# Block-sparse attention and GELU MLP in one kernel: a written-out order, other turns of batch 0's keys and queries, and second-batch loads without holds

## The chip, the cores and the metric

The kernel runs on one core of one Trainium2 chip. The metric is device time in microseconds (us). Instructions are named by their engine: PE (TensorE, matrix products), DVE (VectorE), ACT (ScalarE), POOL (GpSimd) and SP (SyncE, which here only starts transfers). L1124 is line 1124 of the kernel before; the changed file is shorter, and its lines are named only where the text says so.

## The reference

Four batches of eight heads, 768 positions and 64 elements per head go through an attention in which each query sees its own block of 64 keys and the best three others, causally. The rows of all heads then go through an MLP with a tanh GELU.

```python
def _attn_ref(q, k, v):                       # (4, 8, 768, 64)
    k_rep = k.reshape(B, H, n_blocks, block, D).mean(axis=3)      # 12 blocks of 64
    gate_scores = np.einsum('bhsd,bhnd->bhsn', q, k_rep)          # masked causally
    top_idx = np.argsort(gate_scores, axis=-1)[..., -top_k:]      # top_k = 3
    ...                                       # mask: chosen blocks and the own one, causal
    scores = np.where(mask, scale * np.matmul(q, k.transpose(0, 1, 3, 2)), -1e9)
    attn = softmax(scores)
    return np.matmul(attn, v)

def _moe_ref(x, w_in, w_out):                 # x (3072, 512), w_in (512, 2048), w_out (2048, 512)
    h = x @ w_in
    g = 0.5 * h * (1.0 + np.tanh(c * (h + 0.044715 * h * h * h)))
    return g @ w_out
```

## The kernel before

The work is cut into 16 pairs of heads, four pairs to a batch. The program first writes down every step as an `Op` with the engines that may run it, an estimated duration on each, the steps that it depends on, and the buffers that it takes and gives. `Plan.solve` then plays these through in an order of priority (the table `RANK`, one number for each step), chooses engine and buffer, and the instructions are issued in the order that comes out. Each engine runs its own instructions strictly in that order.

The steps of a pair of heads are these.

- `load` and `load_0` bring q, k and v on SP's queue. Usually rows of 64 floats (256 bytes) are read. In the other form, `emit_t` at L427, pieces of 32 floats (128 bytes) are read, laid out so that DVE's stream transpose (L585) can finish turning the tile. Batch 0 uses the first form for k and for the queries of pairs 0 and 1, and the second form for the queries of pairs 2 and 3 (`TURN`); every later batch uses the second form for k and q.
- `pre` makes the turned keys and queries, the sums of the keys of each block, and the gate. In batch 0 a key tile is turned by an ordinary fp32 product with an identity that has two more columns, of ones in each half (`identk`, 130 columns, L566); the two more columns give the block sums, and one multiplication (L603) puts them in place. A query tile is turned by the transposing form of the same instruction (L569, 128 columns). The gate is L693 on PE, followed on DVE by a small transpose and the four lines L716, L725, L726, L730 that choose the blocks. The choice is turned by PE (L762) and copied beside the queries as a mask.
- `heads2` (batch 0) and `heads` (later batches) are the attention: products with the mask in them (L866, L1049), exponentials on ACT (L885, L1062), the causal cut on POOL (L911, L1076), products with v (L934, L1088), division (L953, L972), and a turn of the result into `xT` (L991, L996).

For each batch, `s1` makes the hidden layer (L1124 on PE, GELU on ACT at L1136). For batch 0 `s2_plain` makes the second layer (L1206); for later batches `s2` makes it with seven products in place of eight (L1254). The first product of `s1(0)` needs the first half of w_in and the last exponentials of batch 0.

`load_w` starts the transfers of w_in and w_out, two halves each, on POOL's queue at L485. `hold` is a transfer of 16 elements from a weight tile on SP's queue (L493). SP's queue stops at it until that half of the weights has landed, and so the loads behind it start late: the first hold stands ahead of k and q of pair 4, the second ahead of v of pair 4 and everything of pair 5 and later pairs. On SP's queue each transfer also waits until the eighth transfer before it has landed.

`warm` gives 72 products of an identity with itself (L1401), of lowest priority, which the plan puts wherever it believes PE to be idle.

Of the kernel before, what the change touches and what calls it, by code (L numbers as in the profile page):

```python
# [20 lines left out]
RANK = [  # L21
    143, 420, 146, 147, 145, 418, 121, 260, 475, 56, 260, 228, 112, 261,
    587, 70, 261, 497, 19, 324, 5, 4, 324, 6, 2, 323, 8, 631, 1, 326, 32,
    54, 326, 31, 24, 324, 16, 758, 3, 329, 20, 42, 329, 13, 337, 326, 40,
    367, 372, 329, 30, 355, 38, 955, 1277, 846, 49, 934, 948, 573, 141, 248,
    583, 1191, 645, 590, 118, 241, 117, 242, 240, 198, 61, 119, 83, 613,
    108, 900, 357, 89, 751, 650, 150, 88, 253, 252, 148, 388, 1017, 1315,
    1018, 986, 109, 50, 36, 362, 473, 27, 204, 130, 22, 28, 712, 129, 23,
    21, 832, 236, 135, 265, 286, 124, 209, 428, 151, 520, 230, 325, 351,
    954, 235, 327, 350, 901, 624, 328, 433, 1099, 552, 310, 939, 305, 97,  # L30
    375, 529, 318, 882, 317, 417, 374, 889, 330, 285, 363, 287, 69, 233,
    595, 174, 137, 595, 90, 176, 339, 384, 339, 95, 111, 256, 898, 581, 441,
    280, 110, 897, 629, 923, 227, 474, 352, 298, 258, 543, 921, 62, 259,
    660, 142, 626, 829, 316, 510, 131, 216, 710, 276, 160, 26, 187, 282,
    321, 366, 189, 526, 208, 277, 533, 257, 185, 949, 431, 429, 494, 430,
    577, 331, 268, 641, 278, 838, 381, 625, 273, 289, 320, 462, 237, 465,
    369, 461, 730, 171, 464, 359, 341, 436, 458, 264, 358, 348, 1512, 269,
    456, 364, 398, 937, 213, 432, 361, 365, 360, 864, 460, 251, 219, 639,
    281, 354, 272, 347, 909, 234, 535, 344, 899, 340, 338, 370, 307, 127,
    218, 760, 387, 373, 243, 217, 791, 98, 379, 378, 945, 353, 186, 839,  # L40
    416, 478, 371, 776, 523, 956, 380, 138, 591, 524, 175, 343, 229, 488,
    170, 349, 801, 445, 840, 482, 12, 199, 65, 491, 595, 309, 564, 37, 79,
    85, 80, 84, 713, 17, 1128, 1069, 1232, 283, 284, 1228, 43, 41, 134, 313,
    1093, 1138, 1143, 1171, 755, 9, 559, 314, 400, 579, 288, 477, 466, 476,
    522, 15, 415, 444, 446, 521, 11, 1071, 504, 413, 1094, 25, 585, 512,
    602, 592, 94, 1070, 621, 841, 1072, 7, 593, 530, 528, 642, 14, 489,
    1114, 1319, 484, 10, 578, 414, 409, 485, 39, 493, 471, 454, 499, 18,
    549, 859, 861, 560, 34, 684, 734, 952, 1073, 35, 636, 596, 1102, 677,
    48, 496, 857, 447, 486, 29, 1235, 1257, 1269, 1286, 165, 1248, 778, 990,
    1198, 1220, 1217, 1218, 1223, 308, 203, 291, 211, 190, 715, 721, 1230,  # L50
    51, 172, 1226, 1266, 503, 565, 534, 681, 767, 676, 576, 822, 678, 652,
    653, 759, 770, 786, 612, 536, 911, 787, 792, 793, 800, 916, 917, 1043,
    1249, 126, 125, 222, 293, 295, 303, 292, 300, 226, 158, 689, 690, 736,
    743, 817, 836, 965, 404, 195, 192, 391, 395, 545, 546, 702, 423, 201,
    757, 421, 424, 425, 377, 691, 693, 718, 762, 735, 563, 495, 479, 505,
    541, 519, 619, 1124, 487, 194, 1237, 729, 246, 247, 245, 244, 249, 498,
    584, 427, 383, 604, 795, 794, 1061, 1213, 412, 746, 630, 932, 1321, 440,
    434, 270, 91, 907, 401, 768, 123, 634, 63, 796, 720, 104, 212, 798, 802,
    651, 675, 1040, 72, 724, 896, 46, 1044, 919, 254, 605, 223, 1039, 106,
    615, 294, 667, 744, 178, 668, 774, 924, 597, 68, 1329, 597, 87, 662,  # L60
    597, 173, 205, 52, 53, 81, 82, 77, 396, 76, 773, 989, 531, 86, 78, 918,
    74, 107, 385, 144, 221, 386, 159, 816, 664, 225, 356, 844, 833, 177,
    977, 392, 163, 692, 183, 782, 834, 301, 181, 154, 940, 835, 179, 740,
    393, 164, 705, 402, 538, 890, 335, 599, 103, 156, 599, 115, 169, 599,
    132, 162, 33, 73, 601, 616, 666, 459, 71, 688, 513, 483, 665, 719, 845,
    149, 255, 197, 188, 399, 502, 196, 714, 302, 567, 166, 726, 722, 304,
    206, 622, 75, 394, 506, 128, 717, 716, 306, 224, 765, 723, 290, 220,
    707, 403, 514, 673, 764, 537, 698, 262, 600, 96, 550, 600, 140, 334,
    600, 116, 167, 64, 555, 994, 974, 161, 263, 553, 544, 202, 184, 500,
    501, 728, 297, 59, 210, 279, 518, 152, 312, 1127, 618, 122, 1274, 1216,  # L70
    623, 136, 319, 1214, 406, 1126, 480, 368, 322, 733, 139, 1260, 457,
    1215, 938, 271, 470, 114, 661, 410, 1019, 155, 935, 481, 953, 927, 933,
    1264, 603, 790, 812, 903, 566, 250, 930, 902, 654, 426, 606, 725, 761,
    699, 1666, 872, 1341, 883, 1541, 1060, 1023, 992, 1062, 1645, 928, 904,
    922, 942, 1373, 950, 1063, 1088, 1007, 1178, 711, 685, 814, 819, 1663,
    1542, 92, 448, 905, 1067, 655, 1090, 1101, 1547, 818, 913, 910, 929,
    1394, 1064, 1032, 1029, 1068, 1139, 1056, 1053, 975, 1097, 1182, 468,
    451, 453, 925, 1049, 1013, 1059, 1066, 885, 1006, 1001, 875, 876, 101,
    1225, 914, 1356, 1425, 1275, 1100, 1112, 1255, 1227, 1137, 467, 442,
    881, 912, 1098, 1492, 1494, 1491, 1469, 1579, 1649, 804, 450, 463, 1144,  # L80
    1675, 1766, 1751, 1459, 1605, 1609, 1607, 920, 1689, 1688, 1278, 1389,
    1452, 1468, 1641, 1710, 961, 1680, 1660, 1683, 1697, 967, 737, 749, 100,
    1696, 1754, 1009, 1011, 784, 1031, 1033, 1016, 1025, 1024, 1020, 1132,
    1095, 1045, 1131, 1140, 1146, 1147, 1046, 1221, 1262, 1276, 1263, 777,
    750, 1239, 1241, 1080, 659, 656, 772, 1243, 1083, 695, 979, 57, 779,
    783, 1118, 1160, 754, 1158, 1219, 1298, 1324, 886, 1014, 1440, 1516,
    669, 511, 382, 469, 443, 1209, 570, 753, 868, 1152, 1245, 1314, 703,
    1409, 1538, 1424, 1421, 1461, 1458, 1672, 113, 267, 105, 180, 982, 1771,
    200, 982, 1772, 232, 982, 1775, 342, 299, 58, 60, 207, 67, 539, 93, 828,
    452, 397, 66, 969, 527, 848, 1351, 870, 133, 588, 1642, 1156, 988, 1212,  # L90
    1700, 1606, 991, 1429, 1699, 1698, 1092, 1057, 1010, 1048, 1608, 727,
    1581, 1455, 1578, 1177, 1244, 1532, 1496, 1175, 960, 1602, 936, 617,
    968, 1183, 1366, 1047, 157, 983, 1769, 231, 983, 1768, 756, 983, 1770,
    311, 405, 120, 274, 275, 438, 532, 408, 657, 1234, 492, 906, 435, 542,
    849, 866, 865, 644, 878, 1580, 1206, 1258, 1681, 1390, 1065, 1291, 1701,
    1682, 1194, 1159, 1740, 1026, 1717, 1190, 1419, 1021, 1661, 908, 803,
    1117, 1456, 1106, 1236, 1121, 999, 620, 998, 1089, 996, 1406, 830, 984,
    1773, 558, 984, 1774, 594, 984, 1776, 1489, 411, 437, 1724, 1723, 449,
    407, 873, 877, 884, 1332, 1204, 871, 389, 850, 966, 1005, 419, 895,
    1008, 1353, 1304, 1261, 1224, 1290, 915, 658, 1012, 1203, 1355, 780,  # L100
    1085, 1129, 855, 888, 1240, 1022, 1229, 1523, 1242, 1145, 856, 887, 788,
    1084, 825, 1030, 1289, 860, 1113, 747, 985, 1778, 556, 985, 1777, 540,
    985, 1767, 748, 1331, 1323, 1515, 1514, 1345, 820, 1346, 1526, 957, 962,
    1352, 1326, 731, 853, 1081, 1082, 672, 1252, 607, 1551, 1335, 1015,
    1201, 1561, 507, 1438, 1120, 1256, 1313, 1483, 1125, 1310, 1322, 1312,
    571, 1296, 1325, 1433, 785, 1437, 1119, 1420, 752, 1055, 1155, 1671,
    1259, 1493, 568, 569, 1270, 1272, 1422, 1684, 697, 831, 808, 869, 1611,
    943, 947, 1037, 1036, 1079, 813, 811, 810, 944, 1728, 1674, 1704, 1695,
    1714, 1104, 993, 1096, 1179, 1736, 1115, 1189, 1135, 1136, 1726, 1300,
    1308, 1306, 1318, 1676, 1170, 1168, 1165, 1172, 1721, 1207, 1635, 980,  # L110
    976, 1038, 1111, 1105, 1103, 562, 1233, 1148, 1163, 1281, 1544, 1134,
    1133, 1161, 1166, 1722, 1173, 1002, 1091, 1162, 1693, 1707, 963, 964,
# [55 lines left out]
class Op:  # L168
    def __init__(self, engines, emit, deps, prio, takes=None, gives=(),
# [5 lines left out]
        self.takes = ([] if takes is None else  # L175
                      [takes] if isinstance(takes, tuple) else takes)
        self.gives = gives
        self.lag = lag
        self.end = None


# [98 lines left out]
def kernel(  # L280
# [55 lines left out]
    NK = 3  # L336
# [1159 lines left out]
```

## Time and profile before

| | |
|---|---|
| three runs | 257.35, 258.61, 259.38 us; median 258.61 |
| span of the profiled execution | 257.8 us, granted clock 1.00 |
| PE, DVE, ACT, POOL busy | 250.8, 179.6, 165.2, 86.3 us |
| L1401, the fillers | 72 on PE |
| first and last product of real work on PE | L566 at 5.03 us, L1254 until 254.15 us |
| first L1124 of batch 0 | 39.58 us |
| DMA | 32.63 MB; SP's queue q1 27.62 MB, the weights' queue q0 4.19 MB |

The profile records one execution. The table of times has no separate time for that execution, so its own time is read from the span: the span runs from the first instruction to the last, and the median of the runs is 0.8 us above it. A product on PE is recorded with its way through the array, so that a PE that is called busy can hide idle time of up to a few tenths of a microsecond; the distance from one start to the next shows more. Times inside the span are counted from its start.

### The profile page before, as it was taken

To read this page: it belongs to the slowest core of one execution; us is meant where nothing else is said; L and a number is where in the kernel's file an instruction comes from. 1 tells how busy PE (TensorE), PEld (TensorE's weight loads), DVE (VectorE), ACT (ScalarE), POOL (GpSimd) and SP (SyncE) were. 2 spreads that over 40 slices of the span, in tenths; PEclk is the share of its full clock that TensorE was granted. 3 is DMA by queue.
4 is the path that set the end of the run, shared out by engine and by line. 5 is a ranking of instruction groups with operands and counts; after the bars stand their busy time and mean duration, and the time that the engine had idled before them with its cause. 6 is when DMAs were issued, how large, how long until landed. Compare 5 with 4: busy or idle time off the path is not lost.

```text
span 257.8 us, 6491 instructions
## 1 busy us (share of the span) xinstructions
PE 250.8 (97%) x2530; PEld 174.8 (68%) x2530; DVE 179.6 (70%) x523; ACT 165.2 (64%) x207; POOL 86.3 (33%) x169
## 2 busy tenths in 40 slices
PE   6799999998999999999999999999999999999997
PEld 5676776564556556556678876556778796667886
DVE  2887863318478999999999999997844462227552
ACT  2359688564789996565989587565898953664000
POOL 8754834003355676223043835100143310000000
DMA  8997898999969997899599694222011152000222
GB/s 159 218 152 161 152 215 132 186 225 185 206 132 212 161 196 159 154 188 174 86 206 194 113 215 99 66 69 51 1 75 42 41 104 83 3 0 0 84 81 84
DMA packets 134095, 32.63 MB, mean 127 GB/s; under 512 B 127696, under 2 KB 130096, under 8 KB 134064
## 3 DMA queue, kind: packets, MB, share of 16 engines
q1 hardware_dynamic: 129328, 27.62, 54.5%
q0 software_dynamic: 3136, 4.19, 10.0%
q10 hardware_dynamic: 1600, 0.39, 0.8%
q8 instruction: 20, 0.33, 0.5%
q14 instruction: 11, 0.09, 0.1%
HBM read 27.26 MB, written 6.29 MB: 130 GB/s over the span
## 4 chain that ended last, share of the span: by engine, by line
PE 71%; DMA 11%; DVE 7%; SPq 7%; ACT 2%; issue 2%; POOL 0%; DVEq 0%; ACTq 0%
PE bank L1254 21%; PE wide L1124 18%; PE wide L1049 10%; PE bank L1206 7%; SPq L427 6%; PE bank L1088 6%; DMA ksd<-in_k_dram 5%; DMA w_in<-in_moe_w_in_dram 4%; PE bank L1401 3%; PE bank L693 2%; DMA qsd<-in_q_dram 2%; PE wide L866 1%; ACT at L885 1%; PE bank L566 1%; DVE sel L725 1%
## 5 line engine op out<-in xcount | busy, mean ns | idle before, releaser
L1124 PE MATMUL wide<-xT,w_in 128*128 128x384 f16 x512 | 87.2, 326 | 0.1
L1136 ACT ACTIVATE G<-wide 128x768 f16<-128x768 f32 x64 | 51.8, 810 | 41.7 <-PE wide L1124 41.7
L1124 PEld LDWEIGHTS <-w_in 128*128 128x128 f16 x512 | 49.3, 98 | 33.2 <-issue 1.9
L1062 ACT ACTIVATE at<-wide 128x896 f16<-128x896 f32 x72 | 63.3, 917 | 10.5 <-PE wide L1049 8.1
L1076 POOL TENSOR_SCALAR_AFFINE_SELECT at<-at 128x256 f16<-128x256 f16 x72 | 31.1, 433 | 66.4 <-ACT at L1062 65.9
L1049 PE MATMUL wide<-qT,kT 76*128 76x512 f16 (+3 forms) x192 | 38.7, 305 | 0.0
L393 POOL CAST kT<-k 64x768 f16<-64x768 f32 x21 | 18.1, 862 | 37.4 <-DVE k L585 30.4
L1254 PE MATMUL bank<-w_out,G 128*128 128x256 f16 x216 | 30.0, 272 | 0.0
L1254 PEld LDWEIGHTS <-G 128*128 128x128 f16 x288 | 26.9, 98 | 4.1
L1298 DVE TENSOR_TENSOR osb<-bank,osb 128x512 f32<-128x512 f32 (+1 forms) x38 | 22.5, 596 | 8.8 <-PE bank L1254 8.2
L1206 PE MATMUL bank<-w_out,G 128*128 128x512 f16 x96 | 25.8, 379 | 0.0
L1088 PEld LDWEIGHTS <-at 128*128 128x128 f16 x504 | 21.6, 98 | 4.3 <-POOL at L1076 0.4
L885 ACT ACTIVATE at<-wide 128x1024 f16<-128x1024 f32 (+3 forms) x24 | 20.8, 917 | 5.5 <-PE wide L866 5.4
L1049 PEld LDWEIGHTS <-kT 76*128 76x128 f16 x192 | 17.5, 98 | 9.7
L1088 PE MATMUL bank<-v,at 128*128 128x65 f16 x504 | 23.8, 194 | 0.0
L1254 PEld LDWEIGHTS <-XS 128*128 128x128 f16 x216 | 20.3, 98 | 3.1 <-issue 0.3
L1254 PE MATMUL bank<-TS,XS 128*128 128x256 f16 x144 | 20.6, 272 | 0.0
L585 DVE STREAM_TRANSPOSE k<-ksd 128x768 f32<-128x768 f32 x12 | 11.6, 969 | 10.2 <-DMA ksd<-in_k_dram 10.2
L1194 DVE TENSOR_TENSOR XS<-G 128x768 f16<-128x768 f16 x12 | 6.5, 550 | 15.2 <-ACT G L1136 15.0
L1401 PE MATMUL bank<-ident 128*128 128x256 f16 x72 | 12.8, 302 | 2.1 <-DVE ident L323 2.1
L972 DVE TENSOR_TENSOR xn<-bank,zr 128x384 f16<-128x384 f32 x24 | 13.4, 558 | 0.8
L1206 PEld LDWEIGHTS <-G 128*128 128x128 f16 x96 | 8.7, 98 | 7.6 <-issue 1.0
(97 smaller groups left out, 322.8 us busy)
## 6 DMA issues: line engine op xcount, KB each, us to landing
out_dram<-osb SPq DMA_DIRECT2D x23, 256.0 KB, 2.0
vsd<-in_v_dram SPq DMA_DIRECT2D x26, 192.0 KB, 3.2
qsd<-in_q_dram SPq DMA_DIRECT2D x48, 96.0 KB, 2.5
ksd<-in_k_dram SPq DMA_DIRECT2D x48, 96.0 KB, 2.5
w_in<-in_moe_w_in_dram POOLq DMA_DIRECT2D x2, 1024.0 KB, 10.7
w_out<-in_moe_w_out_dram POOLq DMA_DIRECT2D x2, 1024.0 KB, 12.5
G<-in_k_dram SPq DMA_DIRECT2D x4, 192.0 KB, 4.6
G<-in_v_dram SPq DMA_DIRECT2D x4, 192.0 KB
```

The costliest lines, as they stand in the source:

```text
L393: nc.gpsimd.tensor_copy(out=out, in_=in_)
L885: nc.scalar.activation(out=T["at", u][:, :, 0:n], in_=plan.buf[("st",) + u].rearrange("p (h w) -> p h w", h=2)[:, :, 0:n], func=AF.Exp, bi ...
L1049: nc.tensor.matmul(st[:, x:e], kT16[i][h][0:76, s0:s0 + 128], qT16[i][h][0:76, s0 + (x - cb):s0 + (e - cb)], start=True, stop=True)
L1062: nc.scalar.activation(out=T["at", u][:, 0:n], in_=plan.buf[("st",) + u][:, 0:n], func=AF.Exp, bias=0.0, scale=SCALE)
L1076: nc.gpsimd.affine_select(out=dg, in_=dg, compare_op=ALU.is_ge, fill=0.0, base=0, pattern=[[0, 2], [1, 128]], channel_multiplier=-1)
L1088: nc.tensor.matmul(pvv[:, qc, 0:65], at[:, cb + (qc - jc) * 128: cb + (qc - jc + 1) * 128], v16[i][:, jc, h, :], start=(gi == 0 and jc == ...
L1124: nc.tensor.matmul(hps[:, 512 * e:512 * e + HALF], w_in16[:, ci, (2 * j + e) * 128: (2 * j + e + 1) * 128], T["xT", b][:, ci, HALF * h:HAL ...
L1136: nc.scalar.activation(out=G[:, :, h, j, :], in_=plan.buf["hps", b, j, h].rearrange("p (e w) -> p e w", e=2)[:, :, 0:HALF], func=AF.Gelu_a ...
L1206: nc.tensor.matmul(plan.buf["ops", b, ti], G[:, f % 2, 2 * ti // NC, f // 2, ti % (NC // 2) * 128:ti % (NC // 2) * 128 + 128], w_out16[:, ...
L1254: nc.tensor.matmul(dst[:, HD * h:HD * h + HD], FACT[m][0][:, j, t * 128:(t + 1) * 128], FACT[m][1][:, j, :], start=(clear and j == 0), sto ...
L1298: nc.vector.tensor_tensor(out=dst(), in0=src(), in1=other(), op=ALU.add)
L1401: nc.tensor.matmul(plan.buf["warm", n][:, 0:256], ident16, z, start=True, stop=True)
```

## The change

`RANK` and `Plan.solve` are gone. In their place stand a list of all steps in the order of issue (`ORDER`), a list of the buffers to take (`BUFFER`), and, for 37 steps, ACT, and for 20 steps, POOL, as the engine; every other step runs on the first engine that it names. Of the 72 fillers `ORDER` names 32: 13 ahead of the first product of real work, 19 after it, and none after the last.

The counts of instructions change in these places. Queries of pairs 2 and 3 are loaded in rows of 64 floats and turned by PE (12 products of 128 columns more; two DVE stream transposes and four SP transfers fewer). Keys of pairs 2 and 3 are turned by the transposing form (12 products of 128 columns in place of 12 of 130), and their block sums are made on DVE by four reductions of 128x384 and four multiplications in place of four multiplications. Five of the eight copies of turned keys go from DVE to ACT and one mask copy goes from ACT to DVE; two copies of queries are added on ACT and two on DVE. The two holds are gone; the second half of w_in and w_out now wait for loads of pairs 4 and 5, by a small copy on POOL that reads them.

```diff
-    TURN = {"k": (), "q": (2, 3), "v": ()}
+    TURN = {"k": (), "q": (), "v": ()}
+    KSUM = (0, 1)
...
-                    if key == "k":
+                    if key == "k" and p in KSUM:
                         nc.tensor.matmul(w[:, c * 130:(c + 1) * 130], src,
                                          identk, start=True, stop=True)
                     else:
                         nc.tensor.transpose(w[:, c * 128:(c + 1) * 128], src,
                                             ident32)
...
+                    if p not in KSUM:
+                        half = slice(6 * a, 6 * a + 6)
+                        nc.vector.tensor_reduce(
+                            out=ks[:, half],
+                            in_=plan.buf["wk", p, a][:, 0:HALF].rearrange(
+                                "p (n w) -> p n w", w=64),
+                            op=ALU.add, axis=AXL.X)
+                        for x in into:
+                            nc.vector.tensor_tensor(
+                                out=x[:, :, half], in0=bmask[:, :, 0:6],
+                                in1=ks[:, half].unsqueeze(1).to_broadcast(
+                                    [128, 2, 6]), op=ALU.mult)
+                        return
...
-    def solve(self):
...
+    def run(self):
+        engine = {n: e for e, ops in ENGINE.items() for n in ops}
+        picks = iter(BUFFER)
+        for n in ORDER:
+            op = self.ops[n]
             for kind, key in op.takes:
+                if key not in self.buf:
+                    self.buf[key] = self.kinds[kind][0][next(picks)]
+            op.emit(engine.get(n, next(iter(op.engines))))
...
-    def load_w(name, dst, src, part, deps, prio, after=None):
+    def load_w(name, first, dst, src, parts, prio, after):
         def emit(_):
+            x = const.tile([1, 16], FP32, name=f"after_{name}_{first}")
+            nc.gpsimd.tensor_copy(out=x, in_=T[after][0:1, 0, 0, 0:16]
...
+            for part in parts:
+                nc.gpsimd.dma_start(out=dst[part], in_=view[part])
-    def hold(name, src, dep):
-        def emit(_):
-            x = const.tile([1, 16], FP16, name=f"held_{name}")
-            nc.sync.dma_start(out=x, in_=src[0:1, 0, 0:16])
-        return add({SP: 0.5}, emit, [dep], prio=-1)
...
+    load_w("in", 0, w_in16, moe_w_in, ins[:1], -200, ("v", 3))
+    for p in (HP, HP + 1):
+        for key in ("k", "q", "v"):
+            load(p, key, issued["v" if p == HP else "q", 3 if p == HP else HP])
+    load_w("in", 1, w_in16, moe_w_in, ins[1:], -100, ("q", HP))
+    load_w("out", 0, w_out16, moe_w_out, outs, 40, ("k", HP + 1))
```

The order on each engine changes nearly everywhere. What the text below uses of it is this. On SP the ten loads of pairs 1 to 3 are followed at once by k and q of pair 4, k of pair 5 and v of pair 4, then six of the eight small `fill` transfers, v and q of pair 5, the last two fills, q and k of pair 6, k of pair 7. On POOL the first half of w_in is started after the cast of pair 3's queries and of its v; the second half after 15 of the 17 causal cuts of batch 0; w_out after all 17 and after the cast of pair 4's v. On DVE the stream transposes of k and q of pair 4 and k of pair 5 stand among the last steps of batch 0, ahead of the last copy of `xT`. On PE the gate of pair 4 stands ahead of `s1(0)`, the gate of pair 5 right behind the first two products of the second layer, and attention of pair 4 follows seven products of the second layer after the end of `s1(0)`.

## The prediction

> **What bounds the kernel now.** I read the page first, then the busy time of each engine in stretches of ten us, then the timelines of PE, ACT, DVE and SP where the stretches point.
>
> ```profile
> span 257.8 us, 6491 instructions
> PE 250.8 (97%) x2530; PEld 174.8 (68%) x2530; DVE 179.6 (70%) x523; ACT 165.2 (64%) x207; POOL 86.3 (33%) x169
> ```
>
> PE has the least room. Since its records overlap, I also took the distances from one start to the next: L1124 has 163 ns for 384 columns, L1254 109 ns for 256, L1206 216 ns for 512, each at its smallest value nearly always. From 62 us to 254 us PE therefore has nothing to give but its work. The stretches (busy us of each engine in ten) say where time is left.
>
> ```profile
> 10.00:20.00 10.00, 7.89 (x109) 6.03 (x107) 8.78 (x39) 5.35 (x9) 4.99 (x8) 1.00 1.09 173
> ...
> 50.00:60.00 10.00, 9.34 (x58) 5.39 (x56) 2.66 (x4) 6.44 (x8) 1.51 (x2) 1.00 1.30 213
> 60.00:70.00 10.00, 9.49 (x60) 4.96 (x61) 6.19 (x21) 5.59 (x8) 2.13 (x4) 1.00 1.06 198
> 70.00:80.00 10.00, 10.00 (x106) 5.58 (x104) 7.40 (x25) 8.49 (x12) 6.69 (x12) 1.00 0.76 151
> ```
>
> So the change can win in two places: in batch 0's attention, before the first L1124 at 39.58 us, and in the hole about 60 us. After that the end follows at a fixed distance: last product at 254.15, then one addition, one store and its landing, 3.65 us to the end of the span.
>
> In batch 0's attention no engine is full; ACT, with 24 exponentials, is the longest chain.
>
> ```profile
> 14.20 1.52 ACT L885 ACTIVATE at<-wide 128x512 f16<-128x512 f32 x2
> ...
> 39.43 1.02 ACT L885 ACTIVATE at<-wide 128x1024 f16<-128x1024 f32 x1
> 40.47 1.28 ACT L832 ACT_TABLE_LOAD   x1
> ```
>
> From 14.20 to 40.47 are 26.3 us; the L885 rows in between add up to 20.9, so ACT waits 5.4 us, each time for L866, which waits for a mask. The hole at 60 us is one late load:
>
> ```profile
> 36.30 0.57 SPq L493 DMA_DIRECT2D held_in<-w_in  x1
> 36.91 4.63 SPq L427 DMA_DIRECT2D qsd<-in_q_dram  x4
> 41.59 2.24 SPq L427 DMA_DIRECT2D ksd<-in_k_dram  x4
> ```
>
> ```profile
> 57.31 0.98 DVE L585 STREAM_TRANSPOSE k<-ksd 128x768 f32<-128x768 f32 x1 [10.16 <-DMA ksd<-in_k_dram]
> ```
>
> ```profile
> 60.51 0.48 PE L693 MATMUL bank<-q,ksb 128*32 128x160 f32 x8 [1.18 <-DVE ksb L645]
> ```
>
> The hold keeps SP until 36.30; k of pair 4 is started at 41.59 and lands at 57.3, and PE waits 1.34 us (start to start) for its gate. The packet records tell why it took 14 us: while w_out flows, the two queues take turns one for one (48 to 50 us: 370 packets of 1 KB from q0 and 370 of 128 bytes from q1), where q1 alone moves 1300 packets of 128 bytes per us.
>
> **The change part by part.** I work with the time from the first L1124 to the end, 257.8 - 39.58 = 218.2 us, and with the moment at which it starts.
>
> *Turning.* L566 costs two records of 112 ns for each of 12 products, 2.7 us; L569 has one of 109 ns, so keys of pairs 2 and 3 cost 1.3 us. The 12 new query turns cost 1.3 us. PE gains 0.1 us, in a stretch where it waits anyway: nothing. On DVE two transposes (0.97 each) and five key copies (0.55) go, 4.7 us; two query copies (1.1), a mask copy (0.55) and four reductions come. L628 sums 768 columns in 0.95 us, so half as many take 0.5 (bounds 0.25 and 0.95), 2.0 in all: DVE gains about 1 us. ACT gains work: of its copies five of 0.48 us, 2.4 in all, now stand between the exponentials.
>
> *First exponential.* Before, DVE makes both gate transposes and copies for both halves of pair 0 ahead of L716 at 9.38. After, the first half's gate needs only its own k and q, and runs before the second half's turn of q: 7.4 in place of 8.27. The mask comes 0.8 us earlier; the two copies on ACT between mask and exponential take it no further back. First exponential 13.35 in place of 14.20.
>
> *ACT's chain.* 13.35 + 20.9 + 2.4 = 36.6 without a wait. The first L1124 needs the buffer of the last exponential but one, 0.4 earlier: 36.2. With all 5.4 us of old waits: 41.6. Following the masks, pair 2's is copied at about 25.3 for an exponential that could start at 25.8, so that product and latency leave 0.6 of wait, and pair 3's at 31.1 leaves 0.5. The late waits of 1.2, 0.7 and 0.4 us before L885 came from the queries turned on DVE (L585 at 27.71) and the gate at 30.06; they go. I take 1.5 us: 37.7.
>
> *First half of w_in.* POOL starts it behind the cast of pair 3's queries, which needs ACT's last query copy. On ACT that is after 9.9 us of exponentials and 2.4 of copies: 13.35 + 12.3 + 0.6 of wait = 26.3. Two casts and the small copy (0.82 + 0.84 + 0.19) make 28.2; before, the trigger was at 27.06 and the half landed at 36.28, 9.2 later. I get 37.4, and 0.8 more for q1's packets in between (26 ns beside 173 for one of 2 KB): 38.2. So the weights set the start of `s1(0)`, at 38.2 (36.8 if ACT never waits and nothing is shared): 1.4 us earlier than 39.58.
>
> *Loads without holds.* q1 moves 870 packets of 256 bytes per us. Counted on from 14 us, ten loads are through at 23.4, k and q of pair 4 (3072 packets each) at 28.1, k of pair 5 at 30.5. That is ahead of the weights' first packets, 2 us after their trigger, at about 30. So pair 4's gate moves ahead of `s1(0)` and the 1.34 us go, and another 0.30 at 123 us. Its 0.41 us on PE leave the stretch after the start. What is late next is q of pair 5: it stands behind v of pair 5, both packet for packet against w_in's second half (38 to 44) and w_out (44 to 55). By those rates v is done at 49, q at 56.6, landed at 58.4. Two casts and the rest on DVE (0.98 + 1.1 + 0.2) make 60.8 for a gate that PE reaches at 60.3. Behind it on PE wait the second layer and pair 4's attention. I take 1.0 us with the mask that follows; bounds 0 and 3.5.
>
> *Changes of array form.* Each step into or out of L866 or L693 costs 96 ns from start to start. After the first L1124 the list before has 24 of them, the new one 16: 0.8 us.
>
> *Fillers.* 40 fewer. Those after the last product ended at 256.5, inside the store's landing: nothing. Others stood where PE waited; one less after the first L1124 is 0.1.
>
> The Trainium skill, "TensorE: Matmul & The Clock Gate", Part 1, speaks against dropping fillers: it says that an idle window of about 3.4 us halves PE's clock, and Part 4 adds that transposes don't count as busy. Here the fillers stand 0.213 us apart until 5 us and 0.109 after; the longest wait after that is 1.46 us of idle PE and the pace stays. By the page's rule one lost window would cost an estimated 1.7 us; no run so far shows it.
>
> *Other orders and buffers.* From 62 us I cost them at nothing, because PE's own work covers them; DVE is 94 to 99% busy from 100 to 160 us, and cover lost there would be PE's time.
>
> Sum: 257.8 - 1.4 - 1.6 + 1.0 - 0.4 - 0.8 - 0.1 = 254.5 us of span; plus 0.8 between span and median, 255.3 us. Bounds, as medians: start 36.2 and no new wait, 252.3; start 41.6 and 3.5 of wait, 261.2.
>
> **The rivals.**
>
> *More than that.* ACT waits nowhere, w_in lands in time, q of pair 5 too: start 36.8 and no wait give a median of 252.9. For it: DVE is relieved. Against: masks still pass through DVE's L716 to L730, 2.1 us a pair.
>
> *The stall changes its name.* q of pair 5 lands at 61: 2.5 us more than I took, 257.8, no difference. For it: k of pair 4 crawled in the same way for 14 us. Against: only 0.5 us separates my two times, but q1 is through most of its queue by then.
>
> *Slower: DVE's queue stands before a load.* The stream transposes of k and q of pair 4 and k of pair 5 now precede the last divisions and `xT` copies. If w_in's first packets come before q of pair 4 is through (28.1, thus a trigger before 26), q gets about 100 packets per us until w_in is done and lands at 37. Behind it wait 0.98 + 0.95 + 0.2 for pair 4, then copies and divisions of 3.3 us, so L1124 runs on from 42.4, 4.2 late; k of pair 5 and with it w_out move back by as much, and with w_out1 some 3 us late at its first product the span is 261.7, median 262.5. For it: one-for-one packets. Against: my trigger is 2.2 us too late for it.
>
> *The change does not do what it says*: nothing speaks for it; the counts of instructions show the turns and the missing holds.
>
> **How the numbers follow.** About 1%, or 2.6 us, is what a measurement of this kernel can tell from no change; the limits are 256.0 and 261.2. My forecast (253.5 to 257) has 0.40, more than that 0.15, the stall under another name 0.28, the slower case 0.17 with other orders' losses after 62 us. Of the forecast, 0.05 lies above 256.0; some of the slower case, 0.03, below 261.2. That makes faster 0.50, same 0.36, slower 0.14. The range, 252.3 to 260.0, leaves out the upper part of the slower case and little below.
>
> **What would show it.** Right: first exponential near 13.4, first product of the first layer near 38, no gap of PE over 1 us after it, pair 4's gate ahead of it, w_in landing about 9 us after its trigger. Wrong: a DVE stream transpose that waits for DMA before 42 us; PE waiting at the gate of pair 5 for over 3 us; gaps of PE after 62 us; fillers or turns at the slow pace after 6 us.

## The result and the profile after

The changed kernel takes 270.88 us (median of four runs, 269.58 to 274.18); the kernel before, run beside it, 258.83 (257.35 to 259.38). The ratio is 1.045, with a 95% interval of 1.041 to 1.050: slower by 4.5%, where 255.3 us had been forecast. Ratios and intervals, here and below, are formed from the runs within 1.5% of the fastest of their kernel, while medians and ranges take in all runs. The profiled execution took 270.02 us with a span of 268.3. Lines of the changed kernel are some 40 lower: L1124 is now L1085 (first layer), L1136 is L1097 (GELU), L693 is L654 (gate), L885 is L846 (exponentials), L585 is L533 (stream transpose), `fill` issues at L490.

The page of the changed kernel, its head and two rows of the 40 slices:

```profile
span 268.3 us, 6414 instructions
...
PE 249.2 (93%) x2490; PEld 172.6 (64%) x2490; DVE 177.3 (66%) x524; ACT 167.4 (62%) x213; POOL 86.7 (32%) x169
...
PE   6899999904999999999999999999979999999994
...
PEclk9999999985999999999999999999999999999999
```

PE's busy time fell by 1.6 us; the span rose by 10.5. The loss is idle time, and the slices show it: a zero and a four at 54 to 67 us, a lower clock in the same place, and a seven near 200 us. The stretches of ten us (columns: PE, PEld, DVE, ACT, POOL, clock, DMA share, GB/s) give its size.

```profile
40.00:50.00 10.00, 10.00 (x77) 6.34 (x75) 6.29 (x22) 5.75 (x8) 2.68 (x4) 1.00 0.93 162
50.00:60.00 10.00, 3.79 (x24) 2.15 (x22) 0.00 (x0) 1.55 (x2) 0.00 (x0) 0.91 1.32 187
60.00:70.00 10.00, 6.00 (x24) 3.06 (x24) 1.98 (x4) 3.13 (x4) 0.00 (x0) 0.58 1.02 161
70.00:80.00 10.00, 10.00 (x78) 5.39 (x76) 5.47 (x19) 7.90 (x10) 0.81 (x2) 1.00 0.18 40
```

From 54 to 63 us every engine stands still; only DMA is full. Two rows of the waits name the chain:

```profile
ACT G L1097 <- DMA kT<-G: 11.1, 1, 11.1
...
PE wide L1085 <- ACT G L1097: 10.2, 1, 10.2
```

ACT's timeline shows the GELU that waited. It is the tenth of batch 0, for slice 7 of the hidden units in the second half.

```profile
51.23 0.81 ACT L1097 ACTIVATE G<-wide 128x768 f16<-128x768 f32 x1 [0.49 <-PE wide L1085]
63.13 1.51 ACT L1097 ACTIVATE G<-wide 128x768 f16<-128x768 f32 x2 [11.09 <-DMA kT<-G]
66.75 0.81 ACT L1097 ACTIVATE G<-wide 128x768 f16<-128x768 f32 x1 [2.11 <-PE wide L1085]
```

Why does a GELU wait for a transfer out of G? The block indicators E2 lie in columns of G that are not yet in use (`E2 = G[:, 1, 1, NJ-2:NJ, :]`), and the `fill` transfers read them there. The GELUs of slices 6 and 7 of the second half overwrite these columns, so they wait until the last fill has read. SP's timeline shows where that last pair stood:

```profile
36.98 5.40 SPq L490 DMA_DIRECT2D kT<-G  x6
42.48 4.18 SPq L365 DMA_DIRECT2D vsd<-in_v_dram  x2
46.71 3.21 SPq L377 DMA_DIRECT2D qsd<-in_q_dram  x4
49.96 3.56 SPq L490 DMA_DIRECT2D kT<-G  x2
53.56 10.44 SPq L377 DMA_DIRECT2D qsd<-in_q_dram  x4
```

Six fills are issued at 37 us, the last two at 50, behind v and q of pair 5. q of pair 5 is 3072 packets of 128 bytes, and w_out runs beside it: from 54 to 60 us the packet records hold 1059 packets of 1 KB in q0 and 1056 of 128 bytes in q1, one for one. So the last fill is through at 63 us. In the kernel before, all eight fills were issued between 21.7 and 29.2 us, and no GELU waited:

```profile
21.71 3.23 SPq L542 DMA_DIRECT2D kT<-G  x4
...
26.13 3.03 SPq L542 DMA_DIRECT2D kT<-G  x4
```

w_out itself was late, because POOL triggers it behind the cast of v of pair 4, and that load was late:

```profile
46.39 0.82 POOL L343 CAST v<-vsd 128x768 f16<-128x768 f32 x1 [8.34 <-DMA vsd<-in_v_dram]
...
47.30 1.78 POOL L435 DMA_DIRECT2D w_out<-in_moe_w_out_dram  x2
```

Batch 0's attention went as forecast; these rows of ACT's timeline answer to those at 14.20, 39.43 and 40.47 us before:

```profile
13.46 1.52 ACT L846 ACTIVATE at<-wide 128x512 f16<-128x512 f32 x2
...
35.81 2.21 ACT L846 ACTIVATE at<-wide 128x1024 f16<-128x1024 f32 x3 [0.40 <-PE wide L827]
38.05 1.28 ACT L793 ACT_TABLE_LOAD   x1
```

And there is new idle time late, in the third batch. This is the timeline of all engines, the rows of POOL and of the products that waited:

```profile
193.88 3.93 POOL L1037 TENSOR_SCALAR_AFFINE_SELECT at<-at 128x256 f16<-128x256 f16 x2 [23.64 <-ACT at L1023]
...
197.76 0.82 POOL L343 CAST v<-vsd 128x768 f16<-128x768 f32 x1
...
197.86 0.39 PE L1049 MATMUL bank<-v,at 128*128 128x65 f16 x7 [0.79 <-POOL at L1037]
...
199.54 1.20 POOL L1037 TENSOR_SCALAR_AFFINE_SELECT at<-at 128x256 f16<-128x256 f16 x2
...
200.00 0.39 PE L1049 MATMUL bank<-v,at 128*128 128x65 f16 x7 [0.72 <-POOL at L1037]
```

Two causal cuts take 1.93 and 2.04 us, where the median of all is 0.41; the third comes after two casts (0.82 us each) that the waiting product does not need.

The account, in start-to-start times: the forecast span was 254.5. Take off the 1.0 us for pair 5's gate (PE had stopped before it, and the gate did not wait), add 10.36 for the stop, 2.13 for products that start 0.320 us apart instead of 0.163 behind it, 0.95 and 0.88 for the two late waits and 0.38 for one at 144 us: 268.2, and the profile has 268.3.

### The profile page after: what moved, and what is told of

The parts are those of the page before. It is cut to its first block, busy times and chain, and to the rows that moved or that the text cites. A ratio compares the mean times of both kernels' runs of the same rounds, so it can differ in the third digit from the quotient of the medians.

```text
span 268.3 us, 6414 instructions
## 1 busy us (share of the span) xinstructions
PE 249.2 (93%) x2490; PEld 172.6 (64%) x2490; DVE 177.3 (66%) x524; ACT 167.4 (62%) x213; POOL 86.7 (32%) x169
## 3 DMA queue, kind: packets, MB, share of 16 engines
q1 hardware_dynamic: 126128, 27.62, 53.3%
## 4 chain that ended last, share of the span: by engine, by line
PE 69%; SPq 12%; DMA 10%; POOL 3%; ACT 2%; issue 2%; DVE 0%; POOLq 0%; ACTq 0%
PE wide L1085 27%; PE bank L1217 18%; PE wide L1010 9%; PE bank L1168 8%; SPq L365 8%; PE bank L1049 6%; SPq L377 5%; DMA kT<-G 5%; DMA vsd<-in_v_dram 4%; POOL at L1037 2%; PE bank L654 2%; DMA G<-in_q_dram 1%; ACT at L1023 1%; PE bank L952 1%; ACT G L1097 1%
## 5 line engine op out<-in xcount | busy, mean ns | idle before, releaser
L1085 PE MATMUL wide<-xT,w_in 128*128 128x384 f16 x512 | 91.1, 331 | 10.2 <-ACT G L1097 10.2
L1097 ACT ACTIVATE G<-wide 128x768 f16<-128x768 f32 x64 | 51.8, 811 | 46.7 <-PE wide L1085 35.5
L1085 PEld LDWEIGHTS <-w_in 128*128 128x128 f16 x512 | 49.9, 99 | 43.6 <-issue 13.5
L1037 POOL TENSOR_SCALAR_AFFINE_SELECT at<-at 128x256 f16<-128x256 f16 x72 | 34.0, 486 | 105.0 <-ACT at L1023 104.5
L1217 PE MATMUL bank<-w_out,G 128*128 128x256 f16 x216 | 31.3, 272 | 0.0
L1261 DVE TENSOR_TENSOR osb<-bank,osb 128x512 f32<-128x512 f32 (+1 forms) x38 | 22.3, 593 | 12.9 <-PE bank L1217 10.3
L1217 PEld LDWEIGHTS <-G 128*128 128x128 f16 x288 | 26.7, 98 | 5.0 <-issue 0.3
L1168 PE MATMUL bank<-w_out,G 128*128 128x512 f16 x96 | 27.6, 379 | 0.0
L1049 PE MATMUL bank<-v,at 128*128 128x65 f16 x504 | 25.3, 194 | 1.7 <-POOL at L1037 1.7
L846 ACT ACTIVATE at<-wide 128x1024 f16<-128x1024 f32 (+3 forms) x24 | 20.8, 920 | 2.0 <-PE wide L827 1.8
L533 DVE STREAM_TRANSPOSE q<-qsd 128x768 f32<-128x768 f32 x12 | 11.6, 969 | 15.2 <-DMA qsd<-in_q_dram 15.2
L343 POOL CAST kT<-k 64x768 f16<-64x768 f32 x20 | 16.7, 833 | 3.4 <-DVE k L533 2.5
L343 POOL CAST v<-vsd 128x768 f16<-128x768 f32 x13 | 11.3, 873 | 16.4 <-DMA vsd<-in_v_dram 16.3
L670 DVE STREAM_TRANSPOSE sel<-bank 128x160 f32<-128x160 f32 (+2 forms) x17 | 5.6, 330 | 13.6 <-PE bank L654 13.4
```

The lines of the kernel that those rows point to most:

```text
L343: nc.gpsimd.tensor_copy(out=out, in_=in_)
L846: nc.scalar.activation(out=T["at", u][:, :, 0:n], in_=plan.buf[("st",) + u].rearrange("p (h w) -> p h w", h=2)[:, :, 0:n], func=AF.Exp, bi ...
L1037: nc.gpsimd.affine_select(out=dg, in_=dg, compare_op=ALU.is_ge, fill=0.0, base=0, pattern=[[0, 2], [1, 128]], channel_multiplier=-1)
L1049: nc.tensor.matmul(pvv[:, qc, 0:65], at[:, cb + (qc - jc) * 128: cb + (qc - jc + 1) * 128], v16[i][:, jc, h, :], start=(gi == 0 and jc == ...
L1085: nc.tensor.matmul(hps[:, 512 * e:512 * e + HALF], w_in16[:, ci, (2 * j + e) * 128: (2 * j + e + 1) * 128], T["xT", b][:, ci, HALF * h:HAL ...
L1097: nc.scalar.activation(out=G[:, :, h, j, :], in_=plan.buf["hps", b, j, h].rearrange("p (e w) -> p e w", e=2)[:, :, 0:HALF], func=AF.Gelu_a ...
```

## The experiments

Theory A: the fills hold G, and with it the GELU, ACT and PE. Theory B: the late w_out, or the order as a whole, stops PE, and the fills only end last by chance. Most edits are moves of steps in the list of issue. A helper moves step n ahead of another step when the list is played, with engines and buffers as they were:

```diff
-        for n in ORDER:
+        order = list(ORDER)
+        for n, ahead_of in ((143, 165),):     # last fill pair ahead of v of pair 5
+            order.remove(n)
+            order.insert(order.index(ahead_of), n)
+        for n in order:
```

It makes the file five lines longer, so L1085 is L1090 there and so on. Below only the moves are given.

### The last fills sooner

The diff above.

> The changed kernel, with one step moved in the order: the last pair of fill transfers (kT<-G) is started ahead of v of pair 5 instead of behind v and q of pair 5. Theory A (the GELU that overwrites the indicator columns in G waits for the last fills to have read them, and these stand in q1 behind q of pair 5): the 10.4 us stop of PE at 53.5 us goes, and with it the 2.1 us of cold pace behind it; what is late then is q of pair 5 itself, which lands at 62 to 63 us where its gate is reached at about 60.5 us: a wait of 3 to 5 us. Span 260 to 262, where the changed kernel has 268.3. Theory B (the late w_out, or the order of the work as a whole, stops PE, and the fills only end last by chance): the stop stays within 2 us of its length, span 266 to 268.

Measured: a median of 261.6 us, ratio to the kernel before 1.015 (1.007 to 1.022); span of the profile 258.0, the shortest of four (the others 259.8, 260.0 and 263.0). The stop at 53 us and the slow pace are gone. What is left is the gate of pair 5:

```profile
62.85 0.48 PE L659 MATMUL bank<-q,ksb 128*32 128x160 f32 x8 [2.05 <-DVE ksb L611]
```

From start to start that is 2.21 us, less than the 3 to 5 expected, since in this run v of pair 4 was early and w_out was triggered at 40.03 us. The sum closes: 10.36 + 2.13 - 2.21 is 10.3, and the span fell by 10.3. One step in the wrong place of a list of some 1600 was nearly the whole loss: 10.3 of the 10.5 us between the profiles, 9.3 of the 12.0 between the medians. That is as theory A has it.

### E2 in a tile of its own

```diff
-    E2 = G[:, 1, 1, NJ - 2:NJ, :].rearrange("p a b -> p (a b)")
+    E2 = const.tile([128, 2 * HALF], FP16, name="E2")
```

> The changed kernel with its order untouched; the indicator columns E2 get a tile of their own instead of columns of G, so that no GELU overwrites what the fills read. Theory A: the fills stay as late as they are (issued at 50 us, through at about 62 us), yet the stop at 53.5 us goes; q of pair 5, landing at 62 to 63 us, then holds the gate of pair 5 for 3 to 5 us: span 260 to 262. Theory B: the stop stays, span 266 to 268.

Measured, in one execution: span 264.6. The fills are even later than in the changed kernel (SP's timeline), and ACT runs on at its normal spacing past 60 us:

```profile
47.40 10.21 SPq L377 DMA_DIRECT2D qsd<-in_q_dram  x4
57.66 3.13 SPq L490 DMA_DIRECT2D kT<-E  x2
```

```profile
53.79 0.81 ACT L1097 ACTIVATE G<-wide 128x768 f16<-128x768 f32 x1 [0.49 <-PE wide L1085]
...
60.29 0.81 ACT L1097 ACTIVATE G<-wide 128x768 f16<-128x768 f32 x1 [0.49 <-PE wide L1085]
```

So it is the sharing of G that stops PE, and not the lateness of anything else: theory B falls. The span is 2.6 us above the range that I had expected, because here q of pair 5 came later still, and PE stopped at its gate for 6.83 us and ran slowly again behind that:

```profile
67.36 0.76 PE L654 MATMUL bank<-q,ksb 128*32 128x160 f32 x8 [6.67 <-DVE ksb L606]
```

### Work for PE during the stop

The order is untouched; 80 more filler products stand ahead of the first product that the late GELU holds up.

```diff
-    NWARM = 72
+    NWARM = 120
...
+        at = order.index(405)
+        order[at:at] = range(1851, 1851 + 80)
```

> The changed kernel with 80 additional filler products of 109 ns each (8.7 us of PE) just ahead of the first product that the late GELU holds up, so that PE works through most of the stop. It leaves the wait itself as it is. If the slow pace after the stop (0.325 us for a product of 0.163) comes from PE having stood idle, the products after the stop run at 0.163 at once: 2.1 us less, span about 266.2. If it comes from something else that happens at 64 us, the slow pace stays: span 268.3 or a little more.

Measured, in one execution: span 265.3. Rows of PE's and of ACT's timeline (L1375 are the fillers, L1096 the first layer, L1108 the GELU):

```profile
53.82 8.90 PE L1375 MATMUL bank<-ident 128*128 128x256 f16 x80
63.09 3.09 PE L1096 MATMUL wide<-xT,w_in 128*128 128x384 f16 x18 [0.37 <-ACT G L1108]
...
62.22 1.51 ACT L1108 ACTIVATE G<-wide 128x768 f16<-128x768 f32 x2 [9.99 <-DMA kT<-G]
```

18 products take 3.09 us: full pace at once. The clock in the stretches is 1.00 throughout. The span is 3.0 us lower, of which 0.9 is the stop's own earlier end (63.09 in place of 63.99) and 2.1 the pace. So the slow pace came from PE standing idle. This run says one thing more: v of pair 4 was early in it and w_out was triggered at 40.03 us, 7 us sooner than in the changed kernel, and yet the GELU waited 9.99 us for the fills. That too is against theory B.

The Trainium skill, "TensorE: Matmul & The Clock Gate", Part 1, which the prediction weighed, says that an idle window of about 3.4 us halves the clock. The runs agree: behind stops of 10.4 and 5.7 us the first layer's products start 0.320 us apart in place of 0.163, behind the stop of 6.8 us the second layer's lose the same share, and behind the stop of 2.2 us the pace is kept.

### q of pair 5 sooner as well

The moves are (143, 165) and (162, 165): the last fills and q of pair 5 ahead of v of pair 5.

> As the run with the last fills moved, and q of pair 5 is started ahead of v of pair 5 too. Theory A: no stop at 53.5 us and next to none at the gate of pair 5, since q lands at about 54 to 57 us; v of pair 5 is late instead, and nothing needs it before 70 us. Span 255 to 257.5, so 257 to 259 us with what lies around it: level with the kernel before or 1 us below it. Theory B: stays at 264 or more.

Measured: 263.49 us in the middle of four runs that spread from 258.01 to 266.38. The profiled execution is the longest, with a granted clock of 0.95 from 10 us to its end, so its span isn't compared. Its waits can be read: no stop at 53 us, but 2.75 us of idle PE at the gate of pair 5, because v of pair 4 was late again (cast at 45.75, w_out at 46.78 us). The best run had the span that was expected, 256.3; the others did not. So it was half a miss: something else moved from run to run.

The traces of three versions with the same loads up to v of pair 4 show what. Between the two halves of w_in, at 36 to 38 us, q1 is nearly alone for about 1.5 us and moves 1500 to 2200 packets:

```
packets of q1 from 36 to 38 us   128 bytes (k, pair 5)   256 bytes (v, pair 4)   cast of v, pair 4
changed kernel                   1438                     752                    46.39 us
last fills moved                  514                    1238                    39.12 us
fillers in the stop               489                    1050                    39.12 us
```

Whatever of v does not get through in this gap waits for w_in's second half, and everything behind it waits too.

### w_out ahead of the cast

Moves: as before, and (171, 316): on POOL, w_out's trigger ahead of the cast of v of pair 4.

> The run with the last fills and q of pair 5 started ahead of v of pair 5, and one more step moved: on POOL, w_out is triggered ahead of the cast of v of pair 4 instead of behind it. The two runs with the moved fills spread over 258.0 to 263.0 and 256.3 to 262.1 us of span (without the one at clock 0.949). Theory A2: v of pair 4 gets through either in the 2 us between the two halves of w_in (cast at 39 us, w_out at 40) or only behind the second half (cast at 46, w_out at 47), and w_out, with q of pair 5 beside it packet for packet, moves by the same 7 us. Then w_out flows from 44 us in every run here, q of pair 5 lands by 60 us, the gate of pair 5 waits under 1 us, and the spans lie within 256 to 257, so 257.5 to 258.8 us. Rival: the spread has another cause (the clock, the chip); then it stays at 4 us or more.

Measured: ratio 0.995 (0.992 to 0.998, from seven of ten runs), profiled span 255.7. q of pair 5 is there in time, and nothing holds its gate at 60.56 us:

```profile
57.73 0.98 DVE L538 STREAM_TRANSPOSE q<-qsd 128x768 f32<-128x768 f32 x1 [9.83 <-DMA qsd<-in_q_dram]
```

Seven of the ten spans lie between 255.7 and 257.6; three are at 262.2 to 263.0. So this settles most of it, not all: the rival keeps those three, and none of them was profiled.

### The late order

Moves added: (1469, 1294) on PE, and (1561, 1473) and (1565, 1473) on POOL.

> As the run with w_out ahead of the cast, and three steps of the third batch moved in the order: on PE the second value product of pair 13 stands four products of the second layer later, and on POOL a cast of v and one of keys go behind the third affine_select of pair 13 instead of ahead of it. In the changed kernel PE waits 0.95 and 0.88 us there (196.8 and 199.0 us), because two affine_select took 1.93 and 2.04 us, where the median is 0.41, while DVE's additions ran, and a third stood behind two casts. If those waits are lost time, the span falls by 1.8 us to about 254.5, so 256.2 us, about 1% below the kernel before. If other work only takes their place (the exponentials need the tile that the moved product gives back), it falls by under 0.5 us.

Measured: ratio 0.9895 (0.986 to 0.993), six spans from 254.3 to 256.5, the profiled one 254.3. The profile is 1.4 us shorter than that of the run without these moves; of the 1.83 us of waits, 0.27 is left. The cuts are as slow as they were, but PE has other work meanwhile:

```profile
181.32 4.30 POOL L1042 TENSOR_SCALAR_AFFINE_SELECT at<-at 128x256 f16<-128x256 f16 x3 [23.64 <-ACT at L1028]
...
185.67 0.47 PEld L1054 LDWEIGHTS <-at 128*128 128x128 f16 x14 [0.39 <-POOL at L1042]
185.67 0.60 PE L1054 MATMUL bank<-v,at 128*128 128x65 f16 x14
```

This version is faster than both kernels: 256.6 us where the kernel before has 259.38 beside it. In it v of pair 4 was late too (cast at 47.34 us) and it cost nothing, since w_out no longer stands behind it.

### The old way of turning keys

On top of the last version:

```diff
-    KSUM = (0, 1)
+    KSUM = (0, 1, 2, 3)
```

> As the run with the late order mended, but the keys of pairs 2 and 3 are turned in the old way again (a product with the identity that has two summing columns, 130 columns, where the changed kernel uses the transposing form and four reductions on DVE). PE gets 12 products of 2 x 112 ns in place of 12 of 109 ns, 1.4 us more, and DVE loses 4 reductions of 0.55 us, 2.2 us. Theory (the weights' landing sets the start of the first layer): the first product of the first layer stays at 38.2 within 0.3 us, and the span within 0.3 us of the run without this edit. Rival: the turning form is worth what its parts add up to on PE: 1.4 us slower.

Measured: four spans from 255.3 to 255.5, ratio to the kernel before 0.9905 (0.987 to 0.994); the profiled span is 1.0 us above the run without the edit, the median time 0.5 us, and the spans of the two overlap. My theory falls: the start did move, from 38.08 to 39.11 us. ACT's timeline shows how, with waits that the new form doesn't have at that length:

```profile
18.23 1.02 ACT L851 ACTIVATE at<-wide 128x1024 f16<-128x1024 f32 x1 [0.87 <-PE wide L832]
...
27.76 3.77 ACT L851 ACTIVATE at<-wide 128x1024 f16<-128x1024 f32 x4 [0.53 <-PE wide L832]
```

The longer products stand on PE ahead of the scores for which ACT is waiting: at 16.07 us six of them take 1.61 us where the six of the new form take 0.88, and the scores behind them start at 17.61 us instead of 16.88. At the start of the first layer it is 1.0 us and not the rival's 1.4, so part of the extra work falls where PE waits anyway.

### Fills and q5 ahead of everything

Moves on the version with the late order: the four fill steps (139, 141, 143, 145) ahead of k of pair 5 (159), q of pair 5 (162) ahead of v of pair 4 (156).

> As the run with the late order mended, with all fills started ahead of k of pair 5 (at 27 us), and q of pair 5 ahead of v of pair 4. By the packet rates (1300 of 128 bytes per us alone, 100 beside w_in, 190 beside w_out), the fills are through at 30 us, k of pair 5 at 38 to 40, q of pair 5 at 56 to 58, v of pair 4 at 60. The gate of pair 5, reached at 60.5 us, finds q there: no wait, where 0.4 to 1 us is left without this edit. Span 0.4 us lower or equal. If k of pair 5 lands late instead, DVE's transposes at 42 us wait, and the copies behind it hold PE: 1 to 2 us slower.

Measured: span 262.8, ratio 1.013 (1.008 to 1.019). q of pair 5 (57.75 us) and v of pair 4 (60.01) were there when expected, but k of pair 5 was not, and that cost more than the last sentence of the expectation says. SP issued it only from 33.65 us, three quarters of its packets (2304 of 3072) were through at 40 us, and the rest missed the gap between w_in's halves. These are rows of DVE's and of PE's timeline:

```profile
48.48 0.98 DVE L538 STREAM_TRANSPOSE k<-ksd 128x768 f32<-128x768 f32 x1 [5.95 <-DMA ksd<-in_k_dram]
49.38 0.32 DVE L350 COPY xT<-bank 128x384 f16<-128x384 f16 x1
```

```profile
49.76 2.72 PE L1090 MATMUL wide<-xT,w_in 128*128 128x384 f16 x8 [5.55 <-DVE xT L350]
```

This is the slower rival of the prediction ("DVE's queue stands before a load"), with pair 5's k instead of pair 4's: a transpose waits for its load, the copy of `xT` stands behind it, and PE stops for 5.7 us and then runs cold.

### Fills between k of pair 5 and the rest

Moves: the fills ahead of v of pair 4 (156), with q of pair 5 ahead of v of pair 5 (165) in the first version, and ahead of v of pair 4 (156) in the second.

> As the run with the late order mended, with all eight fill transfers started ahead of v of pair 4, behind k of pair 5 (SP's order: k4, q4, k5, fills, v4, q5, v5). Theory: what spread the runs with moved fills (255.7 to 263.0 us of span in one, 254.3 to 256.5 in the next) is that v of pair 4 sometimes gets stuck behind w_in's second half, and the fills and q of pair 5 with it. The fills are through by 38 us here whatever v of pair 4 does; q of pair 5 still stands behind it. Span 254.3 to 255.5 in most runs, none above 257. Rival: k of pair 5 is what sometimes comes late; then some runs stay near 262.

Measured: ten spans, all from 255.6 to 257.9; ratio 0.994 (0.991 to 0.998). The runs at 262 are gone, which speaks for the theory, though the worst is 0.9 above the bound that I gave. PE stands idle for 1.21 us at the gate of pair 5, because v of pair 4 stands ahead of q of pair 5.

> As the run before it in this list, with q of pair 5 ahead of v of pair 4 as well (k4, q4, k5, fills, q5, v4, v5). In the run that did this with k of pair 5 behind the fills, DVE's transpose of k of pair 5 waited 5.95 us for its load and PE stopped for 5.7 us at 43.9 us; with k5 ahead of the fills again (started at 27.3 us, through in the gap between w_in's halves at 38 us) this stop goes, and q of pair 5 lands by 57 us: no wait at its gate in any run. v of pair 4 lands near 60 us, and its first product is due near 68. Span 254.0 to 254.6 in nearly every run, time 255.7 to 256.3. If 3072 packets of q5 ahead of it make v of pair 4 late instead, PE waits at its first value product: 1 to 3 us slower.

Measured: ratio 0.9885 (0.984 to 0.993), profiled span 254.4, five spans from 254.4 to 255.5, where 254.0 to 254.6 was expected of nearly all, and one of 264.9. The stop at 43.9 us is gone, q of pair 5 is there at 58.05 us for a wait of 0.2, and v of pair 4, cast at 59.39, holds nobody. The one long run was not profiled. Its granted clock was 0.987, as in the run with fills and q5 ahead of everything, where k of pair 5 was late (0.986 and 0.987 at spans of 260.8 to 262.8); the other five have 1.000; so PE probably stopped for long in it too. That k of pair 5 was again the cause is not shown.

### w_in sooner

The moves of the last run, and (147, 51): w_in's first trigger ahead of the cast of v of pair 3.

> As the run before it in this list, with the trigger of w_in's first half moved ahead of the cast of v of pair 3 on POOL, so 0.8 us sooner (27.5 us). If the landing of the weights sets the start of the first layer (landing 8.5 us behind the trigger, first product 1.2 us behind that), the first product moves from 38.1 to 37.3 us and the span falls by 0.8. If ACT's exponentials set it, the start moves by 0.3 at most. If k of pair 5 is cut off by the earlier weights (0.8 us are 1000 of its packets), DVE waits for it at 42 us and the span rises by 3 us or more.

Measured: the trigger comes at 27.62 instead of 28.39 us, and the first product at 38.23 instead of 38.09. The profiled span is 254.4 in both. ACT's last exponentials of batch 0 stand where they stood:

```profile
35.90 2.21 ACT L851 ACTIVATE at<-wide 128x1024 f16<-128x1024 f32 x3 [0.40 <-PE wide L832]
38.13 1.28 ACT L798 ACT_TABLE_LOAD   x1
```

But the run doesn't decide between the two by itself, because the half landed no sooner: at 37.80 us, 37.72 in the run without the move. All twelve profiles from the changed kernel on do decide it. In each the first product starts 0.39 to 0.41 us behind the end of the last exponential but one, while the landing of w_in's first half lies anywhere from 0.08 to 1.20 us before it. So the exponentials set the start of the first layer, and not the weights. Two of the four runs of this version had spans of 261.3 and 267.3, as the third case of the expectation would have it, but neither was profiled.

## Why the prediction was wrong, point by point

**First exponential, ACT's chain, start of the first layer.** Right in size: 13.46 us (13.35 forecast), 1.8 us of ACT waits before L846 (1.5), first product at 38.15 (38.2). But the reason given for 38.2, w_in's landing, was wrong. Triggered at 28.45 (28.2 forecast), the half landed at 36.95, 8.5 us later and not 10, 1.2 us before the first product; and the twelve profiles show that ACT's chain sets the start. That 38.2 came out to 0.05 us was luck, since it was the weights' figure. ACT's own figure in the prediction was 37.7, which waits of 1.8 us bring to 38.0.

**Turning: "nothing".** Wrong by 1.0 us at the start of the first layer (0.5 to 1.0 in the time). The step counted PE's time and found it in a stretch where PE waits. It should have asked who waits for PE there: ACT does, for scores that stand behind the turns. The start came out right all the same, so the gain must lie inside the total for ACT's vanished waits, which had been put down to queries turned on DVE; no run separates the two.

**Pair 4's gate and the old stalls.** Right: the gate runs at 36.31 us ahead of the first layer, and the waits of 1.34 and 0.30 us are gone; in the version with the late order PE has no gap over 0.15 us from the first product to 131 us.

**"k of pair 5 at 30.5."** Wrong: in the changed kernel 1438 of its packets moved at 36 to 38 us. I had counted SP's loads on from 14 us at 870 and 1300 packets per us as if SP issued without pause. SP issued this load from 27.84 to 31.24 us, and w_in's packets began at 30.30. This is why v of pair 4 was caught behind w_in, and w_out's packets began near 49 us where I had assumed 44.

**"What is late next is q of pair 5 ... landed at 58.4."** This is the step that failed. The size was some 2 us too low. The run with the last fills moved has the forecast's order of v and q of pair 5 and w_out triggered at 40.03 us; there DVE starts on q at 60.81 us, and PE waits 2.21 us where I took 1.0, inside the bound of 3.5. (In the runs with starts at 57.73 and 58.56, q stands ahead of v of pair 5.) In the changed kernel, with w_out 5 us later than assumed, q was there at 63.1. But the real fault is that the step asked only who needs q of pair 5, and not what is queued behind it. The two fills stood behind it in the same queue; I had named their place in the order myself, costed them at nothing, and not followed who waits for them. It was written in the code: the GELUs of slices 6 and 7 depend on all fills, and the new order issued the last fills from 49.96 us, where the old one had issued all eight by 29.2. That is 12.5 of the 13.8 us between forecast and measurement.

**Cold pace.** The prediction estimated 1.7 us for one lost window, from the page, and found no place for it. The place was the stop, and the price was 2.13: the half pace lasted for 4.4 us of work, more than one window.

**"Other orders and buffers: nothing."** Wrong by 2.2 us. PE's own work covers other engines only while the chain that feeds PE is ahead of it. At 191 us ACT changes from GELU to exponential just before PE needs the first cut, and there a delay of 1.5 us on POOL is PE's at once.

**The rivals.** The one that ended slower had the right mechanism (a queue standing before a load) at the wrong place; the run with fills and q5 ahead of everything shows it at 43.9 us. "The stall changes its name" describes the run with the last fills moved: 1.64 us of old waits gone, 2.21 of a new one in their place, span 258.0.

## What to carry to other kernels

When a load is moved, list everything behind it in its queue, small transfers first, and for each ask which instruction reads or overwrites what it touches: a tile that lies inside another tile makes a later write wait for an earlier read. Hold SP's order against the moments at which a slow stream starts and stops; a load that just misses such a gap can wait for the whole stream (here v of pair 4: 39.12 or 46.39 us). And when a piece of work falls in a stretch where its engine waits, look whether another engine waits for that engine there before costing it at nothing.

## What the runs showed of the hardware

In the changed kernel the five causal cuts on POOL that lie beside DVE's 16-bit additions (0.34 to 1.64 us of overlap) took 0.61 to 2.04 us; the other 67 have a median of 0.41 and none is over 0.81. In the kernel before, the longest beside an addition took 0.70, and partly it was the addition that grew: beside cuts of 0.41 us at 128.20 and 132.45 us, additions took 0.76 and 0.91 us where 0.55 and 0.68 are usual. The Trainium skill, "SBUF — State Buffer", section "SBUF: two separate sides", says that a DVE instruction with two inputs in SBUF and a GpSimd instruction that reads SBUF exclude each other for the whole instruction; the rows fit that, and no run took the additions away to prove it.

A stop of 2.2 us left PE's pace untouched. After one of 5.7 us it was half for 5.4 us of work, after one of 10.4 us for 4.4, so the stops cost some 2.7 and 2.1 us more than they lasted: the longer stop did not cost more. And the two DMA queues took turns packet for packet although one had packets of 1 KB and the other of 128 bytes (1059 against 1056 from 54 to 60 us). Beside w_out q1 moved 163 to 190 packets of 128 bytes per us, and alone, from 65 to 70 us, 1262 to 1350; so a load of many small packets is slowed most.
